# One phase of 96 matmuls for a block's products, in four stretches ordered through GpSimd memsets, in an RWKV6 + tanh-shrink kernel

## Chip, core and metric

The kernel runs on one core of a Trainium2 chip. The metric is the time of one execution on the device in microseconds. The kernel before was run three times: 547.22, 547.36 and 547.70 us, median 547.36.

## The reference

A linear-attention recurrence (RWKV6) over batch B=4, heads H=8, sequence S=768, head size D=48, and a two-layer net on its output, all in fp32:

```python
for t in range(S):
    cur = einsum('bhd,bhe->bhde', u[None] * k_t, v_t)
    y[:, :, t] = einsum('bhd,bhde->bhe', r_t, state + cur)
    state = w_t[..., None] * state + einsum('bhd,bhe->bhde', k_t, v_t)
x = y.transpose(0, 2, 1, 3).reshape(3072, 384)
h = x @ w_in                       # 384 -> 2048
out = (h - tanh(h)) @ w_out        # 2048 -> 384
```

## The kernel before

**Blocks.** The 3072 tokens are cut into 8 blocks of 384 (`blocks`, batch b, half q = 0 or 1 of the sequence). The main loop (L1216) goes over the blocks. For block i it makes 16 steps f of the net: `first` (L838) is three matmuls into the PSUM tile `hp` and a copy to `h` on ACT; ACT and DVE make `g` of it; matmuls of `Fewer.add` (L966, line L964) or `Second.add` (L914, line L917) take older `g` into the accumulators `acc`. Beside it the loop prepares the attention of block i+1 (`later`), so that its xT is there when block i+1 begins. The attention of block 0 is made ahead of the loop, in `boot` (L1097).

**Attention of a block.** The block is 6 chunks of 64 tokens, in three pairs c with a parity `par`; the 8 heads are four pairs p, with h for the head in the pair. In the array and in PSUM a head, a parity or a half of an output lies at partitions 0 or 64, so that each small matmul uses one quarter of the array: the rows it contracts over (0 to 63 or 64 to 127) and the columns it writes. The output of a chunk is the sum of two products:

- `from_states` (L657, matmul in L676): the state before the chunk by `pre`, 48 matmuls a block, contracted over the rows of head h.
- `from_scores` (L683, matmul in L694): the scores `A` in the chunk by `v`, 48 matmuls a block, contracted over the tokens of parity par.

Both are summed in two PSUM tiles `yp[p % 2]` (`att`), each of two banks, one per parity. A bank and a half of its partitions thus gets sums from one half of the array's rows in `from_states` and, for half of the places, from the other half of the rows in `from_scores`.

**The fence between them.** `result` (L706) opens and closes a part. Behind the first part it issues `nc.tensor.drain().then_inc(fence, 1)` (L716), and ahead of the second part the matmuls wait for that count (L711):

```python
if self.begun and not self.more:
    nc.tensor.wait_ge(fence, len(fences))
...
if not last and not more:
    nc.tensor.drain().then_inc(fence, 1)
```

**Where they stand.** PE, SP, DVE and ACT run in the order in which the code issues (`manual_schedule`, L1067); GpSimd's order is the scheduler's. `plan` (L1018) says in which step f a block's phases are issued: "result 1" is in step 13 while blocks 0 and 1 are worked on, else in step 12. The loop issues for a step: `first`, the elementwise work, then the phases (L1304), among them "result 1" with `from_states` and the drain; then `add_due(now)` (L1334), the accumulations that have come due; then "result 2" (L1335): `from_scores`, `result_out` (L719), four copies from PSUM by ACT, and `fill_holes` (L731), six small DMAs of SP that bring the 16-row pieces of the tile `late` to xT. What the products need: the states from the DVE steps of "update" (L581), the scores from `earlier` (L496) and from `diagonal_in` (L391), both on DVE.

GpSimd has little to do in the loop: two one-column memsets in `post` per block (L418, from `behind`), one memset of states (L1294).

Of the kernel before, what the change touches and what calls it, by code (L numbers as in the profile page):

```python
# [37 lines left out]
F32 = mybir.dt.float32  # L38
# [12 lines left out]
B, H, S, D = 4, 8, 768, 48  # L51
P = 128
L = 64
# [3 lines left out]
NCP = NCH // 2  # L57
# [4 lines left out]
UP = 2  # L62
HALVES = (UP, 0)
ALL = tuple(range(NPAIR))
D2 = 2 * D
DM = H * D
FF = 2048
KC = DM // P
# [57 lines left out]
def kernel(  # L126
# [12 lines left out]
    nc = tc.nc  # L139

    const = ctx.enter_context(tc.tile_pool(name="const", bufs=1))
# [27 lines left out]
    start = const.tile([P, UP * NCH * LP], F32, name="start", tag="start")  # L169
# [16 lines left out]
    def draw(names, cols):  # L186
        nc.gpsimd.memset(mask_all[0:L, cols], 1.0)
        for m in names:
# [5 lines left out]
            else:  # L194
# [8 lines left out]
    A = const.tile([P, 2, NPAIR, NCP, L], F32, name="scores", tag="scores")  # L203
# [4 lines left out]
    states = [states0[:, 0:NPAIR * NCH * L].rearrange("d (p c e) -> d p c e", c=NCH, e=L),  # L208
              const.tile([P, NPAIR, NCH, L], F32, name="states1", tag="states1")]
# [86 lines left out]
    def scratch(ps):  # L296
        return ps.tile([P, 2, BANK], F32, name="att", tag="att")
# [8 lines left out]
    def passed(to, n):  # L306

        by = ident.bitcast(BF16)[:, 0:16]
        for _ in range(n):
            nc.tensor.matmul(to[0:16, 0:16], lhsT=by, rhs=by, start=True, stop=True, skip_group_check=True)  # L310

    fence, fences = tc.alloc_semaphore("fence"), []

    class Block:
# [342 lines left out]
        def from_states(self, yp, slots, first, last, spread=True, cs=range(NCP), apart=False):  # L657
            if apart:
                for n, slot in slots:
                    for p in reversed(slot):  # L660
                        self.from_states(yp, [(n, [p])], first, last, spread, cs)
                return
            St, width = states[self.q], self.width if first else D
            for c in cs:
                for n, slot in slots:
                    for par in range(2):
                        if self.q == 2 * c + par == 0 and not first:
                            continue
                        for p in slot:
                            for h in range(2):  # L670
                                rows = slice(64 * h, 64 * h + D)
                                e0 = 64 * (h ^ (p % 2))
                                n0 = (n * NCP + c) * L
                                states_c = (first_states[rows, p, :, 2 * c + par] if self.halved else
                                            St[rows, p, 2 * c + par, 0:width])
                                self.done = nc.tensor.matmul(yp[p % 2][e0:e0 + width, par, n0:n0 + L], lhsT=states_c,  # L676
                                                             rhs=self.chunk("pre", p, 2 * c + par, spread)[rows],
                                                             start=(first and n == slots[0][0] and c == 0),
                                                             stop=(last and (n, c) == (slots[-1][0], NCP - 1)),
                                                             skip_group_check=True)  # L680
                                self.opened = self.opened or self.done

        def from_scores(self, yp, slots, first, last):  # L683
            for n, slot in slots:
                for p in reversed(slot):
                    for c in range(NCP):
                        for h in range(2):
                            for par in range(2):
                                toks = slice(64 * par, 64 * par + 64)
                                e0 = 64 * (h ^ (p % 2))  # L690
                                f0 = p * D2 + h * D
                                n0 = (n * NCP + c) * L
                                wide = L if self.halved and p == KC - 1 else D
                                self.done = nc.tensor.matmul(yp[p % 2][e0:e0 + wide, par, n0:n0 + L],  # L694
                                                             lhsT=self.v[toks, c, f0:f0 + wide],
                                                             rhs=A[toks, h, p, c, :],
                                                             start=(first and n == slots[0][0] and c == 0),
                                                             stop=(last and (n, c) == (slots[-1][0], NCP - 1)),
                                                             skip_group_check=True)

        def results(self, ps, halved=False):
            self.width = D if halved or isinstance(ps, Kept) else L
            self.yp = [scratch(ps) for e in range(2)]
            self.begun, self.halved, self.opened = False, halved, None

        def result(self, part, pairs, last=False, more=False, **how):  # L706

# [11 lines left out]
        def result_out(self, pairs, copy=None):  # L719
# [8 lines left out]
                    copies.append((copy[h] if copy else nc.scalar.copy)(out=dst[rows], in_=src[rows]))  # L728
            return copies[0]

        def fill_holes(self, engines, which=range(2 * KC)):  # L731
            for n in reversed(which):
                i, h = n // 2, n % 2
                src = 64 * (n // KC) + 16 * (n % KC)
                engines[n % len(engines)].dma_start(out=self.xT[i][64 * h + D:64 * h + 64],
                                                    in_=self.late[src:src + 16, :])
# [24 lines left out]
        def prepare(self, name):  # L761
# [46 lines left out]
        def general(self, ps):  # L808
# [13 lines left out]
            for p0 in HALVES:  # L822
# [9 lines left out]
            self.results(ps)  # L832
            self.result("from_states", ALL, spread=False)
            self.result("from_scores", ALL, True)
            self.result_out(ALL)
            self.fill_holes([nc.sync])

    def first(xT, f, hp):  # L838
        for kc in reversed(range(KC)):
# [178 lines left out]
    def plan(i):  # L1018
# [1 line left out]

        formed_w = {}
        if i == 0:
            phases = {6: ("turn",), 7: ("update",), 10: ("earlier",), 13: ("result 1",)}
# [10 lines left out]
        else:  # L1034
            phases = {3: ("split 2 0",), 4: ("earlier", "split 2 1", "turned 2", "split 0 01"), 5: ("turned 0",),
                      6: ("join 2 0",), 7: ("join 2 1",), 8: ("join 2 2",), 9: ("join 0 02",), 10: ("update",),
                      12: ("result 1",)}
# [6 lines left out]
        if i == 1:  # L1044
            phases = {4: ("split 2 0",), 5: ("split 2 1", "turned 2"), 6: ("split 0 01",),
                      7: ("earlier", "turned 0", "join 2 0"), 8: ("join 2 1",), 9: ("join 2 2", "join 0 01"),
                      10: ("join 0 2",), 11: ("update",), 13: ("result 1",)}
# [25 lines left out]
        return raws[-1][-1]  # L1073

    more_weights.n = 0

    def begin_behind(ins, dma):
        tc.add_manual_dep(dma.ins, ins.ins.name, mybir.DependencyInfo(
            mybir.DependencyClass.Sync, mybir.DependencyReason.DATA))

    def run(ops):
        for op in ops:
# [14 lines left out]
    def boot(ps, pair, blk, later):  # L1097
# [32 lines left out]
        blk.turn_1(ps, h2)  # L1130
        blk.turn_2(h2)
        earlier()
        blk.results(ps, halved=True)
# [23 lines left out]
        third_a, third_b = convert(*raws.pop(0))  # L1157
        run(second_a)
        more_weights(nc.sync)
        blk.results(ps, halved=True)  # L1160
        blk.yp.reverse()
        blk.result("from_states", both[1], apart=True)
        earlier(1, 1)
# [52 lines left out]
    for i, blk in enumerate(blocks):  # L1216
# [9 lines left out]
        for f in range(NF):  # L1226
# [195 lines left out]
```

## Time and profile before

One execution was profiled on its own. Its numbers:

| | |
|---|---|
| median of three runs | 547.36 us |
| the profiled execution | 547.7 us; span 547.7 us, first to last instruction |
| PE busy | 536.6 us, 98% |
| DVE busy | 459.5 us, 84% |
| ACT busy | 403.7 us, 74% |
| GpSimd (POOL) busy | 5.2 us, 1% |
| L676, `from_states` in the loop | 672 records, 7 blocks of 96 |
| L694, `from_scores`, boot included | 768 records, 8 blocks of 96 |
| granted TensorE clock, mean | 0.995 |

How to read it: an fp32 matmul stands in the trace as two records, so 48 matmuls are 96 records. A row of the timeline has the start in us from the span's start, the length from the first record's start to the last one's end, engine, line, operation, output<-inputs, rows\*columns of the array, the moving operand's shape, and the count. The ends of matmuls are modelled (a record of a small matmul stands with some 0.2 us whatever follows it), so the place where PE's time goes is read from starts: from the start of one group to the start of the next. PEld is the loading of weights, and SPq, PEldq are instructions of a queue that do no work on the engine.

### The profile page before, as it was taken

Reading aid. Unit: us, or ns where it says so; the run is one execution under the profiler, and the core shown is the slowest. Engines: PE = TensorE matmul, PEld = TensorE weight load, DVE = VectorE, ACT = ScalarE, POOL = GpSimd, SP = SyncE. Lnnn points to the kernel's source line nnn. Section 1 sums busy time; section 2 is a strip of 40 time slices with the busy share of each in tenths; the row PEclk is TensorE's granted clock in tenths of the full one; section 3 lists DMA queues with packets and bytes.
Section 4 is the critical chain, followed back from the end, with each engine's and each line's share of the span. In section 5 each row is a group of like instructions: output and inputs, shape, how many; then the busy total and the mean of one; then the engine's idle time right before and its main releaser. Section 6 shows DMA issues by size and latency. Waiting matters only on the chain.

```text
span 547.7 us, 14165 instructions
## 1 busy us (share of the span) xinstructions
PE 536.6 (98%) x5730; PEld 404.3 (74%) x5730; DVE 459.5 (84%) x943; ACT 403.7 (74%) x814; POOL 5.2 (1%) x33
## 2 busy tenths in 40 slices
PE   7899999999999999999999999999999999999996
PEld 5756665678777777777777787877778787787874
DVE  7889999999989989789987889879897997557563
ACT  5799996888568876688766886587866885666561
POOL 1100000000000000000000000000000000000000
PEclk9899999999999999999999999999999999999999
DMA  7798632262311632164112532136221410100101
GB/s 274 244 388 318 240 115 81 94 139 64 118 31 64 160 117 56 43 127 136 61 55 85 114 108 68 47 90 158 76 92 48 107 40 3 55 1 0 44 2 47
DMA packets 53046, 56.31 MB, mean 103 GB/s; under 512 B 21488, under 2 KB 50928, under 8 KB 52976
## 3 DMA queue, kind: packets, MB, share of 16 engines
q1 hardware_dynamic: 52592, 55.18, 33.5%
q8 instruction: 46, 0.75, 0.6%
q14 instruction: 24, 0.20, 0.1%
q10 hardware_dynamic: 288, 0.10, 0.1%
q0 software_dynamic: 96, 0.07, 0.1%
HBM read 44.73 MB, written 4.72 MB: 90 GB/s over the span
## 4 chain that ended last, share of the span: by engine, by line
PE 85%; DVE 9%; issue 2%; DMA 1%; ACT 1%; PEld 0%; SPq 0%; PEldq 0%; DVEq 0%
PE hp L840 41%; PE acc L964 27%; PE att L964 6%; PE att L694 2%; PE att L488 2%; DVE w_sb L266 2%; PE acc L917 2%; PE acc L942 2%; PE att L676 2%; PE att L569 1%; DVE s L869 1%; DVE sums L846 1%; DVE h L846 1%; DMA r<-in_rT 1%; DVE post L423 1%
## 5 line engine op out<-in xcount | busy, mean ns | idle before, releaser
L840 PE MATMUL hp<-xT,w_sb 128*128 128x384 f32 x738 | 259.2, 487 | 0.0
L840 PEld LDWEIGHTS hp<-xT,w_sb 128*128 128x128 f32 x738 | 131.9, 190 | 69.2
L964 PE MATMUL acc<-forms,g 128*128 128x128 f32 x954 | 133.7, 276 | 0.5
L843 ACT ACTIVATE h<-hp 128x384 f32<-128x384 f32 x123 | 60.4, 491 | 99.3 <-PE hp L840 98.8
L964 PEld LDWEIGHTS acc<-forms,g 128*128 128x128 f32 x954 | 121.6, 192 | 10.3 <-issue 1.2
L846 DVE SCALAR_TENSOR_TENSOR h<-h,s 128x384 f32<-128x384 f32 x128 | 70.8, 553 | 52.1 <-ACT s L861 51.9
L887 DVE TENSOR_TENSOR g<-g 128x256 f32<-128x256 f32 x265 | 103.4, 420 | 7.9 <-PE acc L964 7.2
L862 ACT ACTIVATE qa<-s,shift 128x384 f32<-128x384 f32 x113 | 69.6, 616 | 3.7
L864 ACT ACTIVATE junk<-s,shift 128x384 bf16<-128x384 f32 x113 | 67.7, 600 | 0.0
L846 DVE SCALAR_TENSOR_TENSOR g<-qa,h 128x384 f32<-128x384 f32 x112 | 61.7, 551 | 1.9 <-DVE h L846 0.5
L861 ACT ACTIVATE s<-h 128x384 f32<-128x384 f32 x113 | 59.1, 523 | 3.5
L964 PEld LDWEIGHTS acc<-w_sb,g 128*128 128x128 f32 x318 | 46.7, 191 | 9.7 <-ACT sums L932 0.3
L964 PE MATMUL acc<-w_sb,g 128*128 128x128 f32 x318 | 53.1, 276 | 0.1
L964 PE MATMUL att<-w_sb,g 128*128 128x128 f32 x212 | 35.5, 275 | 0.0
L964 PEld LDWEIGHTS att<-w_sb,g 128*128 128x128 f32 x212 | 31.1, 192 | 5.3
L999 DVE TENSOR_TENSOR sums<-sums 128x256 f32<-128x256 f32 x84 | 32.9, 408 | 1.7 <-ACT sums L976 1.4
L917 PE MATMUL acc<-w_sb,sums 128*128 128x384 f32 x96 | 33.8, 488 | 0.1
L262 ACT ACTIVATE up<-raw 128x768 f16<-128x768 f32 (+1 forms) x32 | 33.5, 1088 | 0.0
L917 PEld LDWEIGHTS acc<-w_sb,sums 128*128 128x128 f32 x96 | 18.0, 190 | 12.2 <-DVE top L869 0.3
L411 DVE TENSOR_TENSOR_SCAN pre<-w,start 128x780 f32<-128x780 f32 x14 | 25.0, 1783 | 0.5
L423 DVE TENSOR_TENSOR_SCAN post<-w,seed 128x780 f32<-128x780 f32 x14 | 24.9, 1776 | 0.0
L864 ACT ACTIVATION_READ_ACCUMULATOR junk<-s,shift 128x1 f32 x113 | 21.1, 187 | 0.0
(115 smaller groups left out, 530.1 us busy)
## 6 DMA issues: line engine op xcount, KB each, us to landing
raw<-in_weights SPq DMA_DIRECT2D x16, 768.0 KB, 6.6
w<-in_wT SPq DMA_DIRECT2D x7, 780.0 KB, 4.9
k<-in_kT SPq DMA_DIRECT2D x7, 768.0 KB, 4.4
r<-in_rT SPq DMA_DIRECT2D x7, 768.0 KB, 4.7
v_sb<-in_v SPq DMA_DIRECT2D x8, 576.0 KB, 3.8
k<-in_tokens SPq DMA_DIRECT2D x7, 576.0 KB, 3.9
r<-in_tokens SPq DMA_DIRECT2D x7, 576.0 KB, 4.9
out_y<-sums SPq DMA_DIRECT2D x18, 128.0 KB, 1.8
```

The costliest lines, as they stand in the source:

```text
L262: return lambda: nc.scalar.activation(out=to, in_=of, func=AF.Copy, scale=scale, bias=bias)
L423: return nc.vector.tensor_tensor_scan(out=back(t[:, 0:width]), data0=back(self.tile("w")[:, a:a + width]), data1=back(seed[:, 0:width]), i ...
L840: nc.tensor.matmul(hp, lhsT=w_in_sb[:, f, kc, :], rhs=xT[kc], start=(kc == KC - 1), stop=(kc == 0))
L843: return h, nc.scalar.activation(out=h, in_=hp, func=AF.Copy, scale=1.0 / UPSCALE)
L846: return lambda: nc.vector.scalar_tensor_tensor(out=out, in0=in0, scalar=scalar, in1=in1, op0=op0, op1=ALU.mult)
L861: nc.scalar.activation(out=s, in_=h, func=AF.Square)
L862: nc.scalar.activation(out=qa, in_=s, func=AF.Square, bias=shift[:, 4:5])
L864: nc.scalar.activation(out=junk[:, 0:NB], in_=s, func=AF.Relu, bias=shift[:, 5:6], accum_out=excess[:, at:at + 1])
L887: return lambda: nc.vector.tensor_tensor(out=G[:, to:to + 2], in0=two(G, g_at(q, a0), g_at(q, a1)), in1=two(G, g_at(q, b0), g_at(q, b1)), ...
L917: nc.tensor.matmul(acc, lhsT=g[:, j * P:(j + 1) * P], rhs=w_out_sb[:, f, :], start=(f == self.first), stop=(f == NF - 1))
L964: nc.tensor.matmul(to, lhsT=G[:, g_at(q, a), :], rhs=rhs, start=start, stop=stop, skip_group_check=True)
L999: ops.append(lambda op=op, at=at: nc.vector.tensor_tensor(out=at[0], in0=at[1], in1=at[2], op=OPS[op]))
```

## The change

The two products of each of the seven blocks in the loop are issued as one phase, `together`, at the place where `from_scores` stood, behind `add_due`. The matmuls come in four stretches. A set of banks ("cross") is the pair of banks (tile x, parity par = x xor cross); the order is scores into set 0, scores into set 1, states into set 0, states into set 1, 24 matmuls each. Behind the last matmul of each scores stretch stands a memset of one element on GpSimd that waits for it, and the first states matmul into the same set waits for that memset. There is no drain and no fence in the loop any more. The inner order is by n, c, h, x. Where the state is zero (q = 0, chunk 0) the states matmuls are left out, which were issued before: 40 states matmuls in place of 48 in blocks 2, 4 and 6. The general path behind the branch at the end, which is not taken here, uses the same function. `boot` keeps its old parts and fences; only parameters that it didn't use go.

```diff
+    ended_at = const.tile([1, 1], F32, name="ended_at", tag="ended_at")
...
+    def begin_behind(ins, then):
+        tc.add_manual_dep(then.ins, ins.ins.name, mybir.DependencyInfo(
+            mybir.DependencyClass.Sync, mybir.DependencyReason.DATA))
...
+        def together(self, ps):
+            self.results(ps)
+            yp, spread, St, ended = self.yp, isinstance(ps, Kept), states[self.q], {}
+
+            def scores(p, c, h, par):
+                toks = slice(64 * par, 64 * par + 64)
+                return self.v[toks, c, p * D2 + h * D:p * D2 + (h + 1) * D], A[toks, h, p, c, :]
+
+            def from_state(p, c, h, par):
+                rows = slice(64 * h, 64 * h + D)
+                return St[rows, p, 2 * c + par, 0:D], self.chunk("pre", p, 2 * c + par, spread)[rows]
+
+            def stretch(of, cross):
+                first = cross not in ended
+                begun = set()
+                for n in range(UP):
+                    for c in range(NCP):
+                        for h in range(2):
+                            for x in range(2):
+                                p, par = UP * n + x, x ^ cross
+                                if of is from_state and not (self.q or c or par):
+                                    continue
+                                lhs, rhs = of(p, c, h, par)
+                                e0, n0 = 64 * (h ^ x), (n * NCP + c) * L
+                                done = nc.tensor.matmul(yp[x][e0:e0 + D, par, n0:n0 + L], lhsT=lhs, rhs=rhs,
+                                                        start=first and (x, e0) not in begun, stop=True,
+                                                        skip_group_check=True)
+                                begun.add((x, e0))
+                                if not first and len(begun) == 1:
+                                    begin_behind(ended[cross], done)
+                if first:
+                    ended[cross] = nc.gpsimd.memset(ended_at, 0.0)
+                    begin_behind(done, ended[cross])
+
+            for of in (scores, from_state):
+                for cross in range(2):
+                    stretch(of, cross)
+            self.result_out(ALL)
+            self.fill_holes([nc.sync])
...
-            elif name == "result 1":
-                self.results(ps)
-                self.result("from_states", ALL)
-            elif name == "result 2":
-                self.result("from_scores", ALL, True)
-                self.result_out(ALL)
-                self.fill_holes([nc.sync])
...
-            if later and "result 1" in phases.get(f, ()):
-                behind += later.phase(ps_a, "result 2")
+            if later and "results" in phases.get(f, ()):
+                later.together(ps_a)
```

More of the change, by code (lines that the diff above doesn't have):

```diff
@@ L655, in update_any, with from_states @@
                         in1=kvp[:, c % 2, n0:n0 + D], op0=ALU.mult, op1=ALU.add)
-        def from_states(self, yp, slots, first, last, spread=True, cs=range(NCP), apart=False):
+        def from_states(self, yp, slots, first, last, apart=False):
             if apart:
@@ L660, in from_states @@
                     for p in reversed(slot):
-                        self.from_states(yp, [(n, [p])], first, last, spread, cs)
+                        self.from_states(yp, [(n, [p])], first, last)
                 return
-            St, width = states[self.q], self.width if first else D
-            for c in cs:
+            for c in range(NCP):
                 for n, slot in slots:
                     for par in range(2):
-                        if self.q == 2 * c + par == 0 and not first:
+                        if 2 * c + par == 0 and not first:
                             continue
@@ L673, in from_states @@
                                 n0 = (n * NCP + c) * L
[L674 to L681, printed above, removed]
+                                nc.tensor.matmul(yp[p % 2][e0:e0 + D, par, n0:n0 + L],
+                                                 lhsT=first_states[rows, p, :, 2 * c + par],
+                                                 rhs=self.chunk("pre", p, 2 * c + par, True)[rows],
+                                                 start=(first and n == slots[0][0] and c == 0),
+                                                 stop=(last and (n, c) == (slots[-1][0], NCP - 1)),
+                                                 skip_group_check=True)
         def from_scores(self, yp, slots, first, last):
@@ L692, in from_scores @@
                                 n0 = (n * NCP + c) * L
-                                wide = L if self.halved and p == KC - 1 else D
+                                wide = L if p == KC - 1 else D
                                 self.done = nc.tensor.matmul(yp[p % 2][e0:e0 + wide, par, n0:n0 + L],
@@ L699, in from_scores, with results @@
                                                              skip_group_check=True)
[L701 to L704, printed above, removed]
+        def results(self, ps):
+            self.yp, self.begun = [scratch(ps) for e in range(2)], False
         def result(self, part, pairs, last=False, more=False, **how):
@@ L729, in result_out @@
             return copies[0]
+        def together(self, ps):
[11 more added lines that the diff above has]
+                for n in range(UP):
+                    for c in range(NCP):
+                        for h in range(2):
[7 more added lines that the diff above has]
+                                                        start=first and (x, e0) not in begun, stop=True,
+                                                        skip_group_check=True)
+                                begun.add((x, e0))
[9 more added lines that the diff above has]
+            self.fill_holes([nc.sync])
         def fill_holes(self, engines, which=range(2 * KC)):
@@ L831, in general @@
                 self.update_any(ps, p0, self.tots[L])
[L832 to L836, printed above, removed]
+            self.together(ps)
     def first(xT, f, hp):
@@ L1022, in plan @@
         if i == 0:
-            phases = {6: ("turn",), 7: ("update",), 10: ("earlier",), 13: ("result 1",)}
+            phases = {6: ("turn",), 7: ("update",), 10: ("earlier",), 13: ("results",)}
             before = {0: ("behind 2", "take_whole 2"), 2: ("behind 0", "take_whole 0"), 3: ("times_behind 2",),
@@ L1075 @@
     more_weights.n = 0
-    def begin_behind(ins, dma):
-        tc.add_manual_dep(dma.ins, ins.ins.name, mybir.DependencyInfo(
-            mybir.DependencyClass.Sync, mybir.DependencyReason.DATA))
     def run(ops):
@@ L1132, in boot @@
         earlier()
-        blk.results(ps, halved=True)
+        blk.results(ps)
         blk.result("from_scores", both[0])
@@ L1159, in boot @@
         more_weights(nc.sync)
-        blk.results(ps, halved=True)
+        blk.results(ps)
         blk.yp.reverse()
```

4 lines of the change are left out of this document (2 added, 2 removed).

## Prediction

> **What bounds the kernel now.** I read the page first (busy time, then the chain that ended last), then the table of stretches, then PE's timeline around the products.
>
> ```profile
> PE 536.6 (98%) x5730; PEld 404.3 (74%) x5730; DVE 459.5 (84%) x943; ACT 403.7 (74%) x814; POOL 5.2 (1%) x33
> ...
> PE 85%; DVE 9%; issue 2%; DMA 1%; ACT 1%; PEld 0%; SPq 0%; PEldq 0%; DVEq 0%
> ```
> ```profile
> 77.00:83.00 6.00, 5.79 (x201) 4.25 (x201) 6.00 (x10) 4.62 (x10) 0.00 (x0) 1.00 0.41 134
> 83.00:104.00 21.00, 21.00 (x67) 12.38 (x66) 20.53 (x40) 15.28 (x35) 0.00 (x0) 1.00 0.24 78
> ...
> 150.00:520.00 370.00, 369.48 (x3833) 289.07 (x3832) 305.83 (x643) 269.30 (x573) 0.53 (x8) 1.00 0.27 74
> ```
>
> The columns of the last fence are PE, PEld, DVE, ACT and POOL busy, then the granted clock. PE carries 85% of the chain and is busy for 369.48 of 370 us, at full clock. So from 83 us on the time is what PE issues: a microsecond taken from PE's queue is a microsecond of the span, and a wait added on PE costs its length. The one stage that isn't full is 77 to 83 us (5.79 of 6.00), where block 1's products stand; there DVE is busy throughout.
>
> The same step of block 5, as it stands in every later block:
>
> ```profile
> 330.74 2.10 PE L840 MATMUL hp<-xT,w_sb 128*128 128x384 f32 x6
> 332.77 1.56 PE L676 MATMUL att<-pre,states 48*48 48x64 f32 x96
> 334.44 1.15 PE L964 MATMUL acc<-forms,g 128*128 128x128 f32 x8
> 335.44 0.39 PE L964 MATMUL acc<-w_sb,g 128*128 128x128 f32 x2
> 335.66 0.39 PE L964 MATMUL acc<-forms,g 128*128 128x128 f32 x2
> 335.98 1.56 PE L694 MATMUL att<-scores,v_sb 64*48 64x64 f32 x96
> 337.46 2.20 PE L840 MATMUL hp<-xT,w_sb 128*128 128x384 f32 x6
> 339.50 0.27 PE L964 MATMUL acc<-w_sb,g 128*128 128x128 f32 x1
> ```
>
> And a step with no small matmuls in it, with the length of one small matmul and the drain:
>
> ```profile
> 391.95 2.10 PE L840 MATMUL hp<-xT,w_sb 128*128 128x384 f32 x6
> 393.89 0.61 PE L964 MATMUL acc<-w_sb,g 128*128 128x128 f32 x4
> 394.33 1.06 PE L964 MATMUL acc<-forms,g 128*128 128x128 f32 x8
> 395.23 1.13 PE L840 MATMUL hp<-xT,w_sb 128*128 128x384 f32 x3
> ```
> ```profile
> L694 PE MATMUL att<-scores,v_sb x768: 216/216/313, 14.2 to 466.3; 64*48 64x64 f32 x186, 64*64 64x64 f32 x6
> L716 PEldq DRAIN  x9: 462/462/1035, 14.7 to 462.9; - x9
> ```
>
> By starts, an undisturbed `first` takes 1.94 us (391.95 to 393.89) and twelve records of accumulation 1.34 (393.89 to 395.23), 0.11 each. A phase of 96 small records lasts 1.56 less the last one's own 0.22, so 1.34 from first start to last start: 14.1 ns a record. What lies around a phase is the price of having one:
>
> - entry: 2.03 in place of 1.94 (330.74 to 332.77), 0.09;
> - exit without a drain: the last small record starts at 335.98 + 1.34 = 337.32, `hp` at 337.46, 0.14; then `hp` takes 2.04 (337.46 to 339.50) in place of 1.94, 0.10;
> - exit with the drain: last start 334.11, L964 at 334.44, 0.33, so 0.19 for the drain; the twelve records behind it and the next entry take 1.54 (334.44 to 335.98) in place of 1.34, which is again 0.10 and 0.09.
>
> **The change, part by part.**
>
> *Blocks 2 to 7: two phases become one.* Now from `hp` to `hp`: 337.46 - 330.74 = 6.72. Afterwards, with no drain and one entry: `first` 1.94, accumulations 1.34, entry 0.09, one phase of 96 records 1.34 and 96 records more of 14.1 ns 1.35, exit 0.14, in all 6.20. That is **0.52 saved**, and the 0.10 behind the exit stands in both. The rows of the other blocks have the same steps.
>
> *Eight matmuls fewer in blocks 2, 4 and 6* (q = 0): 16 records of 14.1 ns, 0.23; **0.75 saved** in each. Sum of the six blocks: 3 x 0.75 + 3 x 0.52 = 3.81.
>
> *The accumulations move ahead of the products* by some 1.7 us. They need g from DVE. In blocks 2 to 7 what they wait for by the program's order is a step or more old, so they start at once, as L964 does at 393.89 behind `first`. Nothing is lost there.
>
> *Block 1 is another matter.* It has the same order, but the accumulations are L917, and DVE is late:
>
> ```profile
> 75.01 2.10 PE L840 MATMUL hp<-xT,w_sb 128*128 128x384 f32 x6
> ...
> 76.73 0.57 DVE L846 SCALAR_TENSOR_TENSOR sums<-qa,h 128x384 f32<-128x384 f32 x1
> ...
> 77.04 1.57 PE L676 MATMUL att<-pre,states 48*48 48x64 f32 x96
> ...
> 78.72 2.20 PE L917 MATMUL acc<-w_sb,sums 128*128 128x384 f32 x6
> ...
> 79.02 1.94 DVE L391 COPY_PREDICATED scores<-mask_all,diagonal 128x768 f32<-128x768 uint8 x2
> ...
> 81.01 1.56 PE L694 MATMUL att<-scores,v_sb 64*48 64x64 f32 x96
> ...
> 82.50 2.20 PE L840 MATMUL hp<-xT,w_sb 128*128 128x384 f32 x6
> ```
>
> The scores are whole only when the second L391 ends, 79.02 + 1.94 = 80.96, and L694 starts 0.05 later. Until then PE now does `from_states` and L917, and waits little. Afterwards scores stand first, and the 48 states matmuls that filled this time are behind them. L917 may start when L846 ends at 77.30, runs until about 79.3, and PE stands for 1.6 us until 81.01: the first stretch begins with pairs 0 and 1, whose diagonal is the later of the two. DVE's order is unchanged and nothing in it up to there waits for these matmuls, so 81.01 stays. From there 96 records more have to be issued before `hp`: 82.50 becomes 83.85, **1.35 lost**. As PE is full from 83 us on, none of it comes back.
>
> *The memsets.* A states stretch waits for the round trip PE, GpSimd, PE:
>
> ```profile
> 63.68 1.63 PE L488 MATMUL att<-pre,post 48*64 48x64 f32 x96
> ...
> 65.40 0.13 POOL L418 MEMSET post<- 128x1 f32 x2 [43.62 <-PE att L488]
> ```
> ```profile
> 1.73 0.28 POOL masks.py:199 TENSOR_SCALAR_AFFINE_SELECT ident<-ident 128x128 f32<-128x128 f32 x1
> ...
> 2.07 0.58 PE L310 MATMUL att<-ident 128*16 128x16 bf16 x17 [2.07 <-POOL ident masks.py:199]
> ```
> ```profile
> 134.46 0.13 POOL L418 MEMSET post<- 128x1 f32 x2 [16.87 <-ACT ks L546]
> ```
>
> GpSimd starts 0.09 after the last matmul ends (63.68 + 1.63 = 65.31), a memset is at most 0.13, and PE starts 0.06 after GpSimd's end (2.01). With the matmul's own 0.22 that is 0.50 from the start of a stretch's last record. The stretch between has 48 records, 0.68; ahead of the second wait in q = 0 it has 40, 0.56. So the trip is hidden, by 0.18 and 0.06, and I take it at nothing. Behind the waiting matmul stand the rest of the products and all of PE's queue, so this cover matters. Bounds: nothing, or, if a wait that is met late in the phase makes PE start up anew, an entry each: 0.09 + 0.04, times 14, 1.8 us. GpSimd's other instructions in the loop are done long before (the L418 memsets of the last fence stand 8 us ahead of block 2's products, and the next blocks repeat this).
>
> *The order of the matmuls.* States now come in pairs on the same array rows (x = 0 and 1 for one h); L676 alternated rows. The row nearest to the new order is the scores' making, which goes h, then parity:
>
> ```profile
> 300.72 1.63 PE L488 MATMUL att<-pre,post 48*64 48x64 f32 x96
> ```
>
> That is 0.07 more for 96 records than L694. So from nothing to 0.07 in seven blocks, 0 to 0.5 us; below nothing is excluded, as 14.1 ns is the shortest spacing of any 64-wide phase here. I take 0.2, because L676 itself, 48 rows deep, has 1.56 to 1.57.
>
> *ACT and SP.* The four copies now wait for the last matmul of all, while today the first starts before the end:
>
> ```profile
> 147.09 0.48 ACT L728 COPY late<-att 128x384 f32<-128x384 f32 x1 [2.09 <-PE att L694]
> 147.28 2.20 PE L840 MATMUL hp<-xT,w_sb 128*128 128x384 f32 x6
> ...
> 147.97 3.71 SPq L735 DMA_DIRECT2D xT<-late  x6
> ...
> 149.52 0.49 ACT L843 ACTIVATE h<-hp 128x384 f32<-128x384 f32 x1 [0.81 <-PE hp L840]
> ...
> 153.94 1.13 PE L840 MATMUL hp<-xT,w_sb 128*128 128x384 f32 x3
> ```
>
> They start some 0.35 later against PE. ACT had 0.81 idle before the next `h`, which hides it; the six DMAs are issued by 151.7 and needed at 153.94 to 154.6 in the tightest block, and a DMA here lands within 1.9 of its issue (the last is issued at 151.1, so by 153.0). Cost nothing; without that cover 0.35 in each of two blocks.
>
> **Sum.** 3.81 - 1.35 - 0.2 = 2.26 us. The profiled execution has 547.7 and would come to 545.4; it is 0.3 above the median of 547.36, which becomes **545.1**.
>
> **The rivals.**
>
> *GpSimd's answer is late (slower).* Place: the first states matmul of each set. With a trip r, a block waits r - 0.68 at the first; the second is then covered in q = 1 and costs 0.12 in q = 0. The gain is gone from about r = 0.95. At r = 1.2: 7 x 0.52 + 3 x 0.12 = 4.0, 549.1. For it: no row shows a memset that PE waits for in the loop. Against: the rows above, the first of them after 43.6 idle us.
>
> *The wait itself empties the array.* Then 14 entries come back, 1.8 us: 546.9, hardly to be told from no change. This is also the case in which the change doesn't do what it says: the drain goes in name only. For it: 0.50 of 0.56 leaves little. Against: in the program's order L676's third matmul also waits for DVE; that wait is met, and its phase is no longer than the others.
>
> *Block 1's loss is made good.* If something on PE later waited for DVE with 1.35 us to spare, 543.7. Against: 369.48 of 370.
>
> *Loads of weights no longer overlap* in same-row pairs:
>
> ```profile
> L694 PEld LDWEIGHTS att<-scores,v_sb x768: 116/120/200, 14.2 to 466.2; 64*48 64x48 f32 x186, 64*64 64x64 f32 x6
> ```
>
> Exposed once in each of 4 x 24 + 3 x 20 = 156 pairs, 0.12 each gives 18.7 us, 563.8. Against it stands L488, which has such pairs and loses 0.07 a phase. [...]
>
> **How the numbers follow.** Forecast 545.1: 0.79. Made good: 0.04. Waits empty the array: 0.09. GpSimd late: 0.06. Loads: 0.02. A measurement of this kernel tells 0.2%, 1.1 us, from no change, so below 546.3 is faster, above 548.4 slower: faster 0.83, same 0.09, slower 0.08. The order's cost (0 to 0.5) and the spread of runs (547.22 to 547.70) make 544.5 to 545.7 of the forecast; the range reaches to 547.0 for the waits, and its low end is 544.4.
>
> **What would show it.** Right: one group of 192 (176) small records per block with no gap over 0.1 us at the stretch borders; `hp` to `hp` 6.2 (5.97 in q = 0); in block 1 PE idle for some 1.6 us until DVE's L391 ends and `hp` near 83.8; POOL's memsets ending before PE needs them. Wrong: PE idle with POOL as the releaser, a spacing of records over 15 ns, a block 1 that starts its products before 81, or idle PE after 84.

## The result, and the profile after

The changed kernel took **551.37 us** (median of 8 runs, 550.54 to 552.88), the kernel before 547.55 in its 8 runs (547.22 to 550.55). The ratio is 1.0052, 95% interval 1.003 to 1.0075: **slower by 0.5%**, where 0.4% faster was forecast. In the runs whose time and span are both known the time is 1.75 us longer than the span (after: 552.88 and 551.1), so spans are compared with spans here and times with times. By this the profiled execution of the kernel before, with its span of 547.7, stands for a time of some 549.4 (an estimate), 2 us above the median, and not 0.3 as the prediction has it; its gain of 2.26 doesn't depend on that.

In the changed kernel the lines are shifted: `hp` is L870 (was L840), the accumulations are L994 (L964) and, in block 1, L947 (L917), the diagonal's copy is L396 (L391), the products are L756, the memsets L763. First the table of stretches of the changed kernel, with the columns as before:

```profile
77.00:83.00 6.00, 3.17 (x183) 2.63 (x182) 5.87 (x9) 1.76 (x5) 0.18 (x2) 1.00 0.46 134
83.00:104.00 21.00, 20.74 (x69) 12.21 (x69) 16.20 (x28) 13.55 (x30) 0.00 (x0) 0.92 0.26 74
...
150.00:520.00 370.00, 367.68 (x3816) 288.98 (x3817) 305.89 (x645) 269.08 (x572) 1.46 (x18) 1.00 0.27 74
```

PE, which had 0.52 us idle in the last stretch, has 2.32 now, and block 1's stretch is half empty: 3.17 busy of 6.00. The view of waits says on what:

```profile
POOL ended_at L763 <- PE att L756: 139.4, 14, 64.7
...
PE att L756 <- issue: 4.8, 4, 1.7
...
PE att L756 <- DVE scores L396: 1.4, 1, 1.4
```

(Columns: us in all, times, longest.) GpSimd waits for PE 14 times; in the loop PE never waits for GpSimd. DVE's scores cost 1.4 us once, as forecast for block 1. New in the products are four stops by "issue": PE waits for nothing that the profile has an event for. PE's timeline shows where, in blocks 1, 2 and 3:

```profile
78.82 1.56 PE L756 MATMUL att<-scores,v_sb 64*48 64x64 f32 x96 [1.43 <-DVE scores L396]
80.20 1.41 PE L756 MATMUL att<-pre,states 48*48 48x64 f32 x85
83.26 0.42 PE L756 MATMUL att<-pre,states 48*48 48x64 f32 x11 [1.66 <-issue]
83.62 3.11 PE L870 MATMUL hp<-xT,w_sb 128*128 128x384 f32 x6
```
```profile
146.74 1.56 PE L756 MATMUL att<-scores,v_sb 64*48 64x64 f32 x96
...
147.78 0.09 POOL L763 MEMSET ended_at<- 1x1 f32 x1 [10.38 <-PE att L756]
...
148.12 1.07 PE L756 MATMUL att<-pre,states 48*48 48x64 f32 x57
...
148.47 0.09 POOL L763 MEMSET ended_at<- 1x1 f32 x1 [0.60 <-PE att L756]
...
150.26 0.59 PE L756 MATMUL att<-pre,states 48*48 48x64 f32 x23 [1.08 <-issue]
150.78 1.56 PE L870 MATMUL hp<-xT,w_sb 128*128 128x384 f32 x4
```
```profile
208.64 1.56 PE L756 MATMUL att<-scores,v_sb 64*48 64x64 f32 x96
210.01 1.52 PE L756 MATMUL att<-pre,states 48*48 48x64 f32 x96
211.47 2.20 PE L870 MATMUL hp<-xT,w_sb 128*128 128x384 f32 x6
```

Block 3 is what was forecast for all: 192 records without a hole, `hp` 2.83 us after the first of them. In block 2 the stop falls after 57 of the 80 states records, 17 into the second set, 0.4 us after the second memset had ended (148.47 + 0.09 = 148.56; PE stops at 148.97). Both waits were met by then. From record to record the stops are 1.87 us in block 1, 1.29 in block 2, 0.92 in block 4, 1.56 in block 6, 5.65 in all; blocks 3, 5 and 7 have none.

**What they have in common.** Number PE's instructions (with its weight loads an fp32 matmul is four of them: L756 has 672 weight loads and 672 matmul records for the 336 matmuls of the scores). The four stops stand behind number 2241, 3521, 6337 and 9153. All are 193 modulo 256. And the page has among the queues one that carries instructions in packets:

```profile
q8 instruction: 45, 0.74, 0.6%
```

In the trace each of the 45 packets has 16,384 bytes, and there are 11,427 records of PE (matmuls, weight loads and a few others), 254 for each packet. With 256 to a packet, the modulus of the stops, it is 64 bytes an instruction, and 11,427 need 45 packets; the kernel before has 11,532 and, by the same count, its 46. So I take q8's packets for pieces of PE's instructions, 256 in each; this is inferred from the counts. In block 2 the DMA view of 147.70 to 148.97 holds one transfer and no other:

```profile
DMA packets 1, 0.02 MB, mean 13 GB/s; under 512 B 0, under 2 KB 0, under 8 KB 0
## 3 DMA queue, kind: packets, MB, share of 16 engines
q8 instruction: 1, 0.02, 4.7%
```

By the trace's record it runs from 147.88 to 148.84; PE stops at 148.97 and goes on at 150.26, 1.42 behind the landing. In the other three the piece lands at 81.77, 274.46 and 403.93, and PE goes on 1.49, 1.57 and 1.50 later.

The difference of the two spans, 3.4 us, by the starts of `hp`: block 1's products +3.23 (10.72 from its first `hp` to the next in place of 7.49); blocks 2, 4 and 6 +0.69, +0.42, +0.97; blocks 3, 5 and 7 -0.52 each. That is 3.75. The rest is not in the products. Up to block 1, where both kernels issue the same, the execution before is 2.11 longer: 1.10 of it at one place in `boot`, behind PE's instruction 961 (193 modulo 256 again), where PE stops for 1.42 us before and for 0.32 after, and some 1.0 near 24 us, where the clock was granted at one half for 3.4 us. In the execution after it was at one half for as long behind block 1's products (+1.69; the 0.92 in the table above), and 0.1 is at the end. So the change costs 3.75; the medians differ by 3.8.

### The profile page after: what moved, and what is told of

Same layout as the page of the kernel before. It is cut to its first block, busy times and chain, and to the rows that moved or that the text cites. A ratio compares the mean times of both kernels' runs of the same rounds, so it can differ in the third digit from the quotient of the medians.

```text
span 551.1 us, 14091 instructions
## 1 busy us (share of the span) xinstructions
PE 536.8 (97%) x5682; PEld 404.7 (73%) x5682; DVE 459.3 (83%) x943; ACT 403.6 (73%) x814; POOL 6.5 (1%) x47
## 4 chain that ended last, share of the span: by engine, by line
PE 92%; DVE 4%; issue 2%; DMA 1%; SPq 0%; DVEq 0%
PE hp L870 43%; PE acc L994 26%; PE att L994 6%; PE acc L947 5%; PE att L756 4%; PE att L493 2%; PE acc L972 2%; PE att L574 2%; PE att L870 1%; DMA r<-in_rT 1%; PE acc L870 1%; DVE scores L501 1%; DVE first_states L630 0%; DVE pre L416 0%; DVE w_sb L267 0%
## 5 line engine op out<-in xcount | busy, mean ns | idle before, releaser
L870 PE MATMUL hp<-xT,w_sb 128*128 128x384 f32 x738 | 260.1, 489 | 0.0
L870 PEld LDWEIGHTS hp<-xT,w_sb 128*128 128x128 f32 x738 | 132.1, 191 | 69.4 <-issue 0.3
L994 PE MATMUL acc<-forms,g 128*128 128x128 f32 x954 | 133.2, 276 | 0.0
L994 PEld LDWEIGHTS acc<-forms,g 128*128 128x128 f32 x954 | 122.0, 192 | 10.3
L917 DVE TENSOR_TENSOR g<-g 128x256 f32<-128x256 f32 x265 | 103.1, 418 | 7.4 <-PE acc L994 6.5
L994 PEld LDWEIGHTS acc<-w_sb,g 128*128 128x128 f32 x318 | 46.8, 191 | 9.7 <-ACT sums L962 0.3
L994 PE MATMUL acc<-w_sb,g 128*128 128x128 f32 x318 | 53.0, 276 | 0.0
L994 PE MATMUL att<-w_sb,g 128*128 128x128 f32 x212 | 35.5, 275 | 0.0
L994 PEld LDWEIGHTS att<-w_sb,g 128*128 128x128 f32 x212 | 31.1, 192 | 5.3
L947 PE MATMUL acc<-w_sb,sums 128*128 128x384 f32 x96 | 34.6, 498 | 0.2 <-DVE sums L876 0.2
L947 PEld LDWEIGHTS acc<-w_sb,sums 128*128 128x128 f32 x96 | 18.6, 196 | 13.5 <-DVE sums L876 1.1
```

What stands on the lines that cost most here:

```text
L870: nc.tensor.matmul(hp, lhsT=w_in_sb[:, f, kc, :], rhs=xT[kc], start=(kc == KC - 1), stop=(kc == 0))
L917: return lambda: nc.vector.tensor_tensor(out=G[:, to:to + 2], in0=two(G, g_at(q, a0), g_at(q, a1)), in1=two(G, g_at(q, b0), g_at(q, b1)), ...
L947: nc.tensor.matmul(acc, lhsT=g[:, j * P:(j + 1) * P], rhs=w_out_sb[:, f, :], start=(f == self.first), stop=(f == NF - 1))
L994: nc.tensor.matmul(to, lhsT=G[:, g_at(q, a), :], rhs=rhs, start=start, stop=stop, skip_group_check=True)
```

## The experiments

**Theory:** PE's instructions are brought in pieces of 256, as inferred above. A phase of 96 matmuls uses 384 within 2.7 us, 256 of them within 1.80, while in the four stops PE went on 2.39 to 2.94 us behind the start of a piece's transfer. So a phase into which two borders of pieces fall stops at the second. Where the borders lie depends on the number of PE instructions ahead, modulo 256. **Rivals:** the waits on GpSimd, in some way that doesn't show as a wait; the order of the matmuls; block 1's delay, with what follows of it. In e1 to e4 the kernel before took 547.93 us (26 runs), in e5 to e8 547.62 (29 runs). To compare executions without what differs at the start (the clock, the stops in `boot`) I also use L, the time from block 1's first `hp` to the last `hp` of all: 461.25 before, 465.0 after (466.70 less the 1.69 of half clock). The expected spans of e2, e3 and e4 were reckoned from the span of before, 547.7, which holds the 2.11 us named above; where such a span was met, that is luck in part, and L decides.

**e1.** Fewer filler matmuls in `boot` (28 of the small ones less, one large one more, L311 and L304 in the changed kernel), 54 PE instructions less in all; nothing else.

```diff
-        own = blk.own(ps, h1, spare=94, ahead=5, late=6)
+        own = blk.own(ps, h1, spare=66, ahead=6, late=6)
```

> The changed kernel, with 54 PE instructions fewer at the start, where PE has time to spare: 28 tiny warming matmuls (56 instructions) go, one 128x512 warming matmul (2 instructions) comes. Nothing else differs. Theory (instruction supply): PE's instructions come in pieces of 16 KB, 256 instructions, and a phase of 384 instructions in 2.7 us eats one faster than the next can come; it stalls where two borders between pieces lie in one phase. In the trace of the change the border lies 108, 51, 77 and 67 instructions into the phases of blocks 1, 2, 4 and 6, and all of these stall 256 instructions further on, at records 180, 152, 165 and 160; in blocks 3, 5 and 7 it lies at 242, 232 and 222, the next one is behind the phase, and they don't stall. With 54 instructions fewer the places are 162, 105, 131, 121 in blocks 1, 2, 4, 6 (no stall) and 40, 30, 20 in blocks 3, 5, 7: stalls of 0.9 to 1.9 us there, near records 148, 143 and 138, and none in the others. Span 549 to 550.5. Rival (GpSimd's round trip, or a property of the blocks with q = 0, or long runs of small matmuls as such): the stalls stay in blocks 1, 2, 4 and 6 at the same records, span 551.

Measured: 551.68 us, ratio 1.0056 (1.0035 to 1.0078). The stops are gone from blocks 1, 2, 4 and 6 and stand in blocks 3 and 5, which had none; again behind instruction 4801 and 7617, 193 modulo 256. Blocks 3 and 4 in PE's timeline:

```profile
210.65 1.56 PE L756 MATMUL att<-scores,v_sb 64*48 64x64 f32 x96
212.03 0.94 PE L756 MATMUL att<-pre,states 48*48 48x64 f32 x51
213.21 0.88 PE L756 MATMUL att<-pre,states 48*48 48x64 f32 x45 [0.24 <-issue]
214.02 1.24 PE L870 MATMUL hp<-xT,w_sb 128*128 128x384 f32 x3
...
275.15 1.56 PE L756 MATMUL att<-scores,v_sb 64*48 64x64 f32 x96
276.53 1.46 PE L756 MATMUL att<-pre,states 48*48 48x64 f32 x80
277.91 1.56 PE L870 MATMUL hp<-xT,w_sb 128*128 128x384 f32 x4
```

The miss: these stops are short, 0.45 and 0.28, and block 7, where two borders also fall, has none. The pieces explain it. From the start of a piece's transfer to PE going on it is 2.38 to 2.94 us in the ten stops of after, e1, e2 and e6, while 256 instructions of such a phase take 1.80; so the length of a stop follows from when the transfer begins. Here it begins earlier against the phase (at 210.82, 0.17 behind its start; in block 5 at 338.95, 0.09 ahead of it; in block 7 at 465.39, 1.8 ahead), while in the changed kernel's blocks 2, 4 and 6 it begins 1.0 to 1.1 us behind the start. What makes a transfer begin when it does stays open. So two borders in a phase are not enough for a stop; the second piece must also be late.

L is 460.17, 4.8 less than after. The time shows nothing of it, and the span, 551.4, is above the expected 549 to 550.5: in the profiled execution block 1 begins at 79.72 in place of 72.90. A stop of 2.10 us in `boot`, behind instruction 449 (193 modulo 256), is part of that, and the clock was at one half for 17 us there; its mean is 0.984 to 0.996 in most runs of this kernel. The fillers that were taken out or this stop may be the cause of the clock; neither was tested.

**e2.** The other way, 86 PE instructions more:

```diff
-        own = blk.own(ps, h1, spare=94, ahead=5, late=6)
+        own = blk.own(ps, h1, spare=139, ahead=3, late=6)
```

> The changed kernel, with 86 PE instructions more at the start, where PE has time to spare (45 tiny warming matmuls more, two 128x512 ones fewer). Instruction supply: the borders move to 22, 221, 156, 247, 146, 237, 136 instructions into the phases of blocks 1 to 7, so only block 1 (22) can stall, near record 139, by 1 to 1.9 us; the others run through in 2.7 us. Span some 547.7 - 2.3 + 1.5 = 546.9 by the rows of the kernel before. Rival (anything but the instructions' place): stalls as in the changed kernel, four of them, span 551.

Measured: 549.67 us, ratio 1.0036 (1.0012 to 1.006); span 546.9, L 461.64, 0.39 above before, where 0.8 below was expected (the span is met by luck). Of the stops in the phases one is left, in block 1, 1.98 us long; the phases of blocks 2 to 7 run through. A short one (0.28 us) stands just behind block 7's phase, in `hp`, again at 193 modulo 256. Block 1 and block 2:

```profile
79.70 1.56 PE L756 MATMUL att<-scores,v_sb 64*48 64x64 f32 x96 [1.44 <-DVE scores L396]
81.08 0.83 PE L756 MATMUL att<-pre,states 48*48 48x64 f32 x42
83.69 0.99 PE L756 MATMUL att<-pre,states 48*48 48x64 f32 x54 [1.78 <-issue]
```
```profile
146.04 1.56 PE L756 MATMUL att<-scores,v_sb 64*48 64x64 f32 x96
147.42 1.45 PE L756 MATMUL att<-pre,states 48*48 48x64 f32 x80
148.80 0.91 PE L870 MATMUL hp<-xT,w_sb 128*128 128x384 f32 x2
```

The waits, the memsets and the order are those of the changed kernel; only the numbers of the instructions differ. So neither the waits nor the order make the stops.

**e3.** The change without the one phase: states where they were, then the accumulations, then scores, each half in two stretches by sets with the memsets, no drain, no zero states; no shift.

```diff
-            for of in (scores, from_state):
+            for of in ((from_state, scores) if part is None else ((from_state,), (scores,))[part - 1]):
                 for cross in range(2):
                     stretch(of, cross)
...
+            if later and "results" in phases.get(f, ()):
+                later.together(ps_a, 1)
...
-                later.together(ps_a)
+                later.together(ps_a, 2)
```

> The order of the kernel before (states, accumulations, scores, two phases apart) in the new stretches by bank sets, with the GpSimd memsets in place of drain and fence, and without the zero states. Instruction supply: no phase has more than 192 instructions and the accumulations lie between, so no stall inside a phase; saved are the drain, 0.19 in each of 7 blocks, and 0.23 in each of 3: 2.0 us, 545.7 for a span of 547.7 before. Block 1 keeps its cover for the late scores. Rival (the wait for GpSimd costs something by itself, 0.13 at each of 14 places): 547.5, with gaps at the first matmul of each scores stretch.

Measured: 547.13 us, ratio 0.9983 (0.9967 to 0.9998); span 544.3, L 459.98, 1.27 below before, where 2.0 was expected. No stop of this kind in the loop. Block 2 of it:

```profile
140.49 1.48 PE L758 MATMUL att<-pre,states 48*48 48x64 f32 x80
141.90 0.71 PE L998 MATMUL acc<-w_sb,g 128*128 128x128 f32 x4
142.45 1.06 PE L998 MATMUL acc<-forms,g 128*128 128x128 f32 x8
143.43 1.56 PE L758 MATMUL att<-scores,v_sb 64*48 64x64 f32 x96
```

From the first states record to the first accumulation it is 1.41 us, in the kernel before 1.67 (332.77 to 334.44): the drain is saved, and of the eight matmuls left out nearly nothing (the 80 records start within 1.26, 96 within 1.345: 0.085). No memset is waited for in these 80 records, so the memsets are not what keeps the rest from being saved.

**e4.** Block 1 as in e3, blocks 2 to 7 in one phase, and the shift of e2.

```diff
+            if later and "results" in phases.get(f, ()) and not i:
+                later.together(ps_a, 1)
...
-                later.together(ps_a)
+                later.together(ps_a, None if i else 2)
```

> The changed kernel with block 1 alone in the order of the kernel before (states, accumulations, scores, without drain) and the 86 instructions more at the start of the second experiment. Instruction supply and the sum of the prediction both hold: block 1 loses nothing to the late scores, blocks 2 to 7 run through without a stall and save 0.52 and 0.75 each: span some 543.9. Rival: four stalls of 1 to 1.9 us in blocks 1, 2, 4, 6, near 549.5.

Measured: 546.08 us, ratio 0.9944 (0.9922 to 0.9966), span 544.2, L 458.48: **faster than both kernels**. By L it is 2.77 below before, where 3.8 was expected. No phase has a stop; behind block 7's phase `hp` has one of 0.41 us, as in e2. Block 1's products wait 0.44 for DVE, beside the accumulations and not behind them:

```profile
76.25 1.56 PE L758 MATMUL att<-pre,states 48*48 48x64 f32 x96
77.74 2.20 PE L951 MATMUL acc<-w_sb,sums 128*128 128x384 f32 x6
80.38 1.56 PE L758 MATMUL att<-scores,v_sb 64*48 64x64 f32 x96 [0.44 <-DVE scores L396]
81.86 2.20 PE L874 MATMUL hp<-xT,w_sb 128*128 128x384 f32 x6
```

**e5.** The control: the kernel before with e2's line in `boot`.

> The kernel before with the same 86 PE instructions more in boot as the shifted kernels have. If those kernels gain by where the borders of the instruction supply fall, this one does not gain: its small phases of 96 records (192 instructions) are shorter than a piece of 256, and stand as before: 1.35 us each, no gap over 0.1 us, 461.3 us from block 1's first hp to the last hp (before 461.25), a median within 0.2% of before. If the padding itself helps (a warmer start, another clock), it gains as the shifted ones did, and the ratio is below 0.997.

Measured: 548.41 us, ratio 1.0022 (1.0004 to 1.0041), L 461.31. The padding itself gains nothing, it rather costs a little, and the loop's phases of 96 records keep their 1.34 to 1.36 us wherever the borders fall (one of fourteen has 1.43). In `boot` there are two stops, 0.45 and 0.54 us, behind instructions 705 and 961.

**e6.** e4 without the shift: block 1 repaired, the borders in blocks 2 to 7 where the change had put them.

> The changed kernel with block 1 issued in two parts (states, accumulations, scores) and no shift: the borders fall in blocks 2 to 7 as in the changed kernel. Supply theory: block 1 loses neither its 1.35 us to DVE nor its 1.87 us gap (two phases of 1.35, no gap), while blocks 2, 4 and 6 keep gaps of some 1.3, 0.9 and 1.6 us at their records 152, 165 and 160; 462.3 us from block 1's first hp to the last hp (458.5 with the shift), a median of some 549. Rival, that the gaps come of the GpSimd waits or of what follows block 1's delay: without that delay blocks 2, 4 and 6 have no gap or another one, 458.5 us, median 546.

Measured: 548.39 us, ratio 1.0017 (1.0001 to 1.0033); L 461.29, 2.8 more than e4. Blocks 2, 4 and 6 stop at the same instructions as after (3521, 6337, 9153), for 1.15, 1.12 and 1.00 us, 3.27 in all where 3.8 was expected. Block 2:

```profile
141.82 1.56 PE L758 MATMUL att<-scores,v_sb 64*48 64x64 f32 x96
143.19 1.07 PE L758 MATMUL att<-pre,states 48*48 48x64 f32 x56
145.20 0.60 PE L758 MATMUL att<-pre,states 48*48 48x64 f32 x24 [0.94 <-issue]
```

Block 1's delay is thus no cause of the others.

**e7.** e4 (with 84 instructions of shift, since drains count too) with one drain between scores and states in place of the memsets.

```diff
-                if first:
-                    ended[cross] = nc.gpsimd.memset(ended_at, 0.0)
-                    begin_behind(done, ended[cross])
...
+                if ended:
+                    nc.tensor.wait_ge(fence, len(fences))
+                drained = not ended
                 for cross in range(2):
                     stretch(of, cross)
+                if drained:
+                    nc.tensor.drain().then_inc(fence, 1)
+                    fences.append(None)
```

> The fastest kernel so far (block 1 split, shifted) with one drain and the fence's wait between the first two stretches and the last two in place of the memsets. If the memsets' round trip is hidden and costs nothing, each of the seven blocks pays the drain: 0.33 us from the last record ahead of it to the next in place of 0.014, or 0.19 at block 1; some 2.1 us in all, 460.5 us from block 1's first hp to the last hp in place of 458.5. If the memsets cost PE something that the gaps don't show, it is as fast or faster: 458.5 or less.

Measured: 548.13 us, ratio 1.0014 (0.9999 to 1.0029); L 460.53, 2.05 more than e4, as expected. From `hp` to `hp` blocks 2 to 6 are each 0.33 to 0.35 longer than in e4; block 1, where PE waits for DVE anyway, doesn't pay, it is 0.21 shorter. Ahead of block 7's first `hp` the stop of e4 is there too, 0.73 us long in place of 0.41. So the drain costs here what was expected; that the sum over all blocks is met too is in part chance. The memsets show no such cost: in the changed kernel it is 0.03 to 0.04 us from record to record at each border of stretches, and up to 0.07 inside a stretch of block 3.

**e8.** e4 with another order of the states in blocks 2, 4 and 6.

```diff
+                if of is from_state and not self.q:
+                    mixed = [s for two in zip(places(0, (0,), (1,)), places(1, (0,), (0,))) for s in two]
+                    stretch(of, 0, places(0, (1, 2)) + mixed[:1])
+                    stretch(of, 1, mixed[1:] + places(1, (1, 2)))
+                    continue
```

(`places(cross, cs, xs)` lists a set's matmuls for pairs cs and tiles xs.)

> The fastest kernel so far, with the states matmuls of blocks 2, 4 and 6 in another order: 16 of set 0, then the eight of chunk pair 0 of both sets in turn, then 16 of set 1, so that all four quarters of the array take turns throughout. Theory: a quarter takes a small matmul each 113 ns (8 records of 14.1), and the eight matmuls left out saved only 0.07 us a block because two quarters alone had work in their place. Then a phase takes 2.46 us instead of 2.62, at most 0.03 of it lost to the memset's trip (17 matmuls of 28 ns are 0.48, the trip is 0.50): 458.0 to 458.1 us from block 1's first hp to the last hp in place of 458.5. Rival, that an eighth more or less of the records costs by itself at the borders of stretches: 2.62 as before.

Measured: 545.74 us, ratio 0.9964 (0.9946 to 0.9981), L 457.94. A phase starts its 176 records within 2.54 us, in e4 within 2.62; 2.46 was expected. So the order matters, but it explains only half of what the eight matmuls failed to save; the other half stays open. That L fell as far as expected is chance: 0.23 of the 0.54 are these three phases, 0.21 a shorter stop behind block 7's phase, 0.09 block 1.

## Why the prediction was wrong

The step that failed is the sum of blocks 2 to 7, "**one phase of 96 records 1.34 and 96 records more of 14.1 ns 1.35**", and block 1's "96 records more have to be issued". The 14.1 ns were measured on phases of 96 records and carried over to 192. Those need 384 instructions of PE, and PE did not have them in time. The stops are 5.65 us, against a forecast gain of 2.26: -2.26 + 5.65 = 3.4, of the measured 3.8; most of the rest is in the terms below, a gain of 2.0 in place of 2.26. Shown by e1, e2 and e6: the same code stops or runs through by where it lies modulo 256, and all ten stops in the phases of after, e1, e2 and e6 stand at number 193 modulo 256, 1.3 to 1.6 us behind the landing of a piece. That PE waits for the piece is inferred from these times; the trace has no event for it, and why PE goes on only so long behind the landing stays open. No rival of the prediction had this. Its list of what would show it wrong had the sign (idle PE after 84) but no cause for it.

Point by point:

- *Blocks 3, 5 and 7, 0.52 each:* right, 0.52 (e2: 0.523, 0.518, 0.522).
- *Blocks 2, 4 and 6, 0.75 each:* mis-sized. Without stops 0.59 (e2: 0.592, 0.599, 0.589). Of the 0.23 for eight matmuls only 0.07 came, so time did not fall with the count. The 14.1 ns a record were measured where all quarters of the array have work, which the first chunk pair has not once its zero states are left out; by e8 the order of these matmuls makes about half of the miss, and the other half stays open.
- *Block 1, 1.35 lost:* right. PE stood 1.43 us until DVE's scores, and 10.72 less 1.86 of stop is 8.86, 1.37 over 7.49; in e1, without a stop there, it is 1.30. What was missing is the stop behind it.
- *The memsets hidden:* right (POOL's rows above: the second memset of block 2 had ended 0.4 us before PE stopped; e7).
- *The order of the matmuls, 0.2:* nothing in blocks 3, 5 and 7. Block 3's 192 records start within 2.685 us, 14.06 ns each. In blocks 2, 4 and 6 the order costs at least the 0.08 that e8 took back.
- *ACT and SP nothing:* right; from block 2 on the two steps behind each phase are as long as before, 3.38 and 3.28 us from `hp` to `hp`. The 1.9 us to a landing in its reading is the median of 45 DMAs, not a bound; the longest took 5.1.
- *Loads that don't overlap:* didn't come, as L488 had said: block 3's 192 records with their loads of 0.12 us start 14.06 ns apart.

Could the profile before have shown it? Yes, with one row. Its page has 46 instruction packets for the whole span, one per 12 us on average, and the new phase asks for one and a half in 2.7. And what a late piece costs stands in the table of groups of the same trace (the last columns are the idle time ahead of such a group's instructions, and what ended it):

```profile
L488 PE MATMUL att<-pre,post 48*64 48x64 f32 x768 | 13.6, 221 | 1.2 <-issue 1.2
```

This is the stop in `boot` named above, in the kernel before: from 19.54 to 20.96 in the middle of a group, behind instruction 961, with PE going on 1.52 us behind the landing of a piece at 19.43. No phase of 192 records stands there. So a long phase was not needed for this stop; the piece's transfer had begun at 18.51, 1.03 us ahead of it, and PE went on 2.44 behind that start. The sum of the prediction has no term for it.

Without any stop the change would have gained 3.34 in blocks 2 to 7 (three of 0.52 and three of 0.59), less 1.37 in block 1, 2.0 us where 2.26 were forecast. e4 shows that block 1 needn't have lost more than 0.16 us.

## What to carry to other kernels

Count instructions as well as time: here 192 records of small matmuls took 2.69 us in blocks 3, 5 and 7, and 4.65 in block 1, where a stop of 1.87 fell among them. Where a change joins two dense stretches on PE, look in the trace for the packets that carry instructions, and see how many the joined stretch uses (here 384 instructions, one and a half packets, in 2.7 us) and how long behind a packet PE goes on (here 2.4 to 2.9 us from the start of its transfer). An idle time in the middle of equal instructions, without a releaser, is worth following up even where it stands once (here 1.2 us at L488). And a step that is good in six blocks is not thereby good in the seventh: the one block whose inputs came late was better left as it was.

## What the hardware showed that was not expected

- The trace's queue q8 moves packets of 16,384 bytes, by the counts 256 of PE's instructions each, 0.9 to 1.6 us in transfer in the changed kernel, and PE went on 1.32 to 1.57 us behind the landing in the ten stops. Such a stop cost 0.28 to 1.99 us in the ten, up to 2.10 in `boot` (e1).
- A stop showed as "issue" on PE and PEld, with no releaser, in the middle of a group of equal instructions (changed kernel, L756: PE 4.8 us and PEld 5.4, four times each).
- Adding 86 instructions of fillers far ahead, of which the loop knows nothing, changed the loop's time by 2.8 us (L of e6 and e4: 461.29 and 458.48).
- The drain in a phase of small matmuls cost 0.33 us in e7 (0.346 from record to record there, where the mean spacing is 0.014). The memsets of GpSimd (14 of 0.09 us) that PE's later matmuls wait for cost none: nothing waited for them in the changed kernel's trace, with 24 other matmuls (0.68 us), or 20 in q = 0, between. With 17 (e8) there was no gap either: PE was busy for 370.00 us of 370 from 150 to 520.
